# A sign step tied to its function table, two more parts of the second product in seven instead of eight, and a re-dated plan

## The chip, the cores and the metric

The program runs on one core of a Trainium2 chip. Its time is device microseconds of one execution, the median of several runs. A core has five engines that matter here: TensorE (PE, the matrix multiplier; PEld is its weight load), VectorE (DVE), ScalarE (ACT), GpSimd (POOL) and SyncE (SP), which issues the DMA transfers. Each executes its own instructions strictly in the order in which they were written down, and waits on semaphores of the others.

## The reference: what is computed

```python
# attention with random features, per batch b (8) and head (8): 576 tokens, 64 wide, 128 features
phi(x) = exp(proj - |x|^2/2 - max) / sqrt(m),  proj = x @ omega.T
kv  = phi(k).T @ v ;  z = sum of phi(k)
attn = (phi(q) @ kv) / (phi(q) @ z + 1e-6)          # -> x: 4608 tokens x 512
# feed-forward
h   = x @ w_in                                      # 512 -> 2048
g   = h * erf(softplus(h))
out = g @ w_out                                     # 2048 -> 512, float32
```

## The kernel before

**Precision.** The two products of the feed-forward part are done in a short float format whose rounding is undone by splitting: every operand is written as high + low, and each product is three matmuls (high·high, high·low, low·high).

**Tiling.** The 4608 tokens are cut into six groups ("supers", line 32, `SUPERS`): two of 2 x 288 tokens and four of 2 x 432. A super passes GEMM 1 (512 to 2048), the nonlinearity, and GEMM 2 (2048 to 512) in four parts q = 0..3 (`NQ`). A part has two granules of GEMM 1's output, each 4 blocks (two feature blocks by two token halves). The names of the trace: `h`, or `hX hY hZ`, are GEMM 1's accumulators, `hs` its output in SBUF, `gs` what softplus and erf make of it, `gh` and `gl` the high and low part of g, `o`, or `oX oY oZ`, GEMM 2's accumulators and `os` its sums. A digit pair behind a name, as in `o_2_3`, is the part and the output block.

**Seven or eight products.** A 2 x 2 block product takes eight products of blocks, or seven with sums of blocks made beforehand (`PRODUCTS`, the accumulators X, Y and Z). GEMM 1 uses eight in the two small supers and seven in the others. GEMM 2 uses seven where `blocked(b, q)` (line 69) says so: super `b` at or past `FIRST2[q]`, and not the last part of the last super. `FIRST2` is 3 for every q, so super 2 and the two small ones use eight. A part in seven products needs four sums of activations (`gsum`, tiles `gs<-hs,hs` and `gs<-hs,gs`), three and a half high/low splits of a granule (`bh bb th`, `bl bb tl`) where a part in eight needs two (`gh`, `gl`), and sums of weights. These are made once, by `make_sums` (tiles R, S, c), in the super ahead of `FIRST2[q]` (line 927: `if b == FIRST2[q] - 1`), stored to DRAM as `wdc`, and fetched as `wb<-wdc` with the plain weights `wb<-wdw`.

**Weights.** They come as 64-bit words and are decoded on the chip, 32 units of them, during the first small super and early in the second (`make`): `wload` (tile st), `pbias` (line 438) on ScalarE (tile wt: a Prelu that makes sign and exponent; "the sign step"), `ptail` and `pjoin` on VectorE, and the split into high and low (tile w).

**Nonlinearity.** `chain` writes for a part: softplus of two granules, erf of the two, and the gate (g = erf · h). ScalarE holds one function table at a time: softplus, erf, and exp with ln (attention) are three sets. So a part takes three table loads: softplus, erf, and exp again.

**What sets the order.** `build` lists all steps with their reads, writes, engines and estimated costs. `Plan.order` (line 150) plays them in estimated time and writes each engine's instructions down in the order found: of the ready steps of an engine, the one with the earliest date (`due`). A step's `set` names the table it needs; while a softplus–erf pair runs (`macro`, `lock`) no other step *with* a set is let in, but one without a set may be. `JITTER` moves the dates of all steps in a stretch of dates by a pseudo-random amount of an entry's size (`o.id` and the entry's number k are the seed). `LAG`, `AHEAD`, `DRAIN`, `DIVIDE`, `GATES`, `RESTS`, `LATE`, `SQA`, `WHG`, `FIRST` and `BY` are numbers by which dates and the choice of engine are set. All instructions carry the source line L1015 (L1047 in the changed kernel), the line of the recorder.

Of the kernel before, what the change touches and what calls it, by code (L numbers as in the profile page):

```python
# [20 lines left out]
B, H, S, D = 8, 8, 576, 64  # L21
# [41 lines left out]
            ("Y", "S4", "B22", (0, 1), 1),  # L63
            ("X", "A22", "T4", (1, 0), 0))

FIRST2 = (3, 3, 3, 3)


def blocked(b, q):

    return FIRST2[q] <= b < len(SUPERS) - (q == NQ - 1)


COST = dict(mm=0.132, proj=0.222, half=0.156, tr=0.109, kv=1.35, table=1.3)
BANDWIDTH = 270e3
LAG = {"T": 0.32725, "A": 0.2525, "V": 0.2605, "G": 0.3105, "S": 0.2904}
SLOTS = dict(w=8, g=11, u=2, f=2, mx=3, sq=3, v=1, qh=1, ql=1, kh=1, kl=1, xs=12, xh=2, xl=2,
             os=4, ps=8)
CAPS = dict(st=3, wt=1, ws=1, wp=2, cv=2, att=4, moe1=5, moe2=3, hs=4, gs=2, w=6, wsums=7)
# [26 lines left out]
class Plan:  # L106
# [43 lines left out]
    def order(self, slots, caps):  # L150
# [6 lines left out]
        for o in reversed(ops):  # L157
# [2 lines left out]
            for s in o.succ:  # L160
                due = min(due, s.due - dur - 0.4)
            o.due = due
        for k, (lo, hi, amp) in enumerate(JITTER):
            for o in ops:
                if lo <= o.due < hi:
                    o.due += amp * ((o.id * 7919 + k * 104729 + 17) % 1009 / 504.0 - 1.0)
# [45 lines left out]
        while True:  # L212
# [74 lines left out]
            while True:  # L287
                if kind == "idle":
                    idle[x] = True
                elif kind == "done":  # L290
                    for s in x.succ:
                        s.left -= 1
                        lag = 0.0 if x.eng != "S" and len(s.opts) == 1 and s.opts[0][0] == x.eng \
                            else LAG[x.eng]
                        s.ready = max(getattr(s, "ready", 0.0) if s.left >= 0 else 0.0, now + lag) \
                            if hasattr(s, "ready") else now + lag
                        if not s.left:
                            event(max(now, s.ready), "push", s)
                    event(now + LAG[x.eng], "free", x)
                elif kind == "free":  # L300
# [17 lines left out]
def whole_(n):  # L318
# [1 line left out]
    return n < WHOLE or WHOLE2[0] <= n < WHOLE2[1]  # L320


JITTER = ((0, 0, 0), (186.1, 206.1, 4), (0, 0, 0), (0, 0, 0), (0, 0, 0), (227.5, 727.5, 4),
          (648.5, 748.5, 1), (712.0, 762.0, 2), (574.9, 594.9, 8), (27.8, 47.8, 0.5), (390.5, 440.5, 8),
          (458.1, 558.1, 8), (876.3, 896.3, 2), (0, 0, 0), (616.6, 816.6, 1))
AHEAD = 40.56

SPANS = ((0, 288), (288, 288))

DRAIN = 2.0  # L330
DIVIDE = 4.0
WHOLE = 32
WHOLE2 = (0, 0)
LESS = []
ROWS = 8
PAIR = 8.0
FIRST = 11.5
LEAD = 30.0
START0 = 4 * FIRST + 5

GATES = 10.0
RESTS = 6.0
EARLY = (0, 0)
STARTS = ()
BY = 30.0
RPOOL = SPOOL = "g"
VOS = 5
TAIL = [("V", 0.69, -1e9)]
LATE = 40.0
LOADS = 1e9  # L350
GATES0 = 1e9
RESTS0 = 1e9
SQN = 4
SQG = -1e9
SQA = 4.0
WHG = 5.0
WBG = -1e9


def build(emit):  # L360
# [49 lines left out]
    def fetch(u, t, src, ks, n):  # L410
        pl.op("wfetch", [("S", 0.1, AHEAD)], lambda e: E.fetch(t.ap[:, ks[0]:ks[-1] + 1].bitcast(F32), src()),
              reads=[(stored[u], 0)], writes=[(t, (x, k)) for x in "hl" for k in ks],
              size=P * n * BW * 8)
# [17 lines left out]
    def make(u, t):  # L431

        nm = "_".join(str(c) for c in u)
        st = pl.tile("w", f"st{nm}", [P, HW, 2], I32, "st")
        pl.op("wload", [("S", 0.1, AHEAD)], lambda e: E.w_load(st, u),
              writes=[(st, "h"), (st, "l"), (t, "room")], size=P * HW * 8)
        w = pl.tile("ps", f"wt{nm}", [P, HW], I32, "wp")
        pl.op("pbias", [("A", 0.67, -1e9)], lambda e: E.w_bias(e, st, w),
              reads=[(st, "h")], writes=[(w, 0)])
        pl.op("ptail", TAIL, lambda e: E.w_tail(e, st), reads=[(st, "l")], writes=[(st, "l")])  # L440
        pl.op("pjoin", [("V", 0.68, -1e9)], lambda e: E.w_join(st, w), reads=[(st, "l"), (w, 0)],
              writes=[(w, 0)])
        parts(t, lambda: w.ap.bitcast(F32).rearrange("p (k c) -> p k c", k=2), [(w, 0)], True)
        store(u, t)

    def room():
        count[0] += 1
        if clock[0] < starts[SUMS]:
            return CAPS["w"]
        return CAPS["wsums"] if clock[0] < starts[max(SUMS + 1, *FIRST2)] else SLOTS["w"]  # L450

# [453 lines left out]
    def gemm2(b, q, et):  # L905
# [16 lines left out]
        def one(t, f):  # L922
            if not ops:
                ops.extend(pl.tile("ps", f"o{b}_{q}_{et}_{i}", [P, 512], F32, "moe2",
                                   6 if b == len(SUPERS) - 1 else None) for i in range(2))
                w.append(weights2(q // 2, et, q % 2))
                if b == FIRST2[q] - 1:
                    beside[q, et] = w[0]
# [448 lines left out]
```

## Time and profile before

| what | value |
|---|---|
| runs | 1026.77, 1027.0, 1029.63 us; median 1027.0 |
| profiled execution | 1027.2 us, span of its instructions 1025.4 us |
| granted TensorE clock, mean | 0.997 |
| busy share of PE, DVE, ACT, POOL | 98%, 78%, 67%, 60% |
| moved by DMA | 232.72 MB, mean 227 GB/s |

How to read it: a busy share is an average over the span, and ends of matmuls are modelled, so what PE loses is seen best in the waits listed against it and in the start-to-start distance of its matmuls. In the rows of a timeline the first number is the start in microseconds from the span's start, the second the time up to the end of the merged instructions, and the bracket the idle time before, with what ended it. In rows of windows the numbers are busy microseconds of PE, PEld, DVE, ACT and POOL (instructions in brackets), the granted clock, the DMA share and GB/s. In rows of groups the number behind the bar is busy time, and behind the comma the mean of one in ns.

By the trace the first small super's GEMM 1 runs from 46.3 to 172 us, the second's from 185 to 332 us, super 2 starts at 345.9 us with its `hX`, super 3's first `hX` is at 502.9 us, and super 2's last `o` matmul at 567 us.

### The profile page before, as it was taken

How to read it: one execution, taken by the hardware profiler on the slowest of the kernel's cores; microseconds unless marked ns; L12 is line 12 of the kernel's file. 1: busy time of each engine (PE TensorE's matmuls, PEld its weight loads, DVE VectorE, ACT ScalarE, POOL GpSimd, SP SyncE). 2: the span in 40 equal slices, each digit the busy share in tenths (PEclk: the TensorE clock that was granted, in tenths of full speed). 3: DMA queues.
4: the chain of work that ended last, by engine and by line, in shares of the span. 5: the costliest groups of instructions: out<-in, count | busy, mean ns of one | idle time of the engine just before them, and what ended most of it. 6: DMA issues, size and time to landing. Idle time of an engine off the chain costs nothing.

```text
span 1025.4 us, 19428 instructions
## 1 busy us (share of the span) xinstructions
PE 1003.5 (98%) x7132; PEld 932.8 (91%) x7132; DVE 795.0 (78%) x1284; ACT 688.5 (67%) x1295; POOL 612.9 (60%) x446
## 2 busy tenths in 40 slices
PE   8999999999999999999999999999999999999998
PEld 7799889999999999999999888989989999989997
DVE  5788878877876976677787987798887687678664
ACT  8988776787685774765768585677657655644650
POOL 3625443875567816455788356489884668957520
PEclk9999999999999999999999999999999999999999
DMA  8377776699686766676657866656786457686751
GB/s 229 90 267 237 255 239 244 240 320 307 218 298 205 255 213 220 225 243 202 223 187 277 280 224 214 226 199 212 246 278 223 164 185 227 219 288 219 230 180 70
DMA packets 99486, 232.72 MB, mean 227 GB/s; under 512 B 11200, under 2 KB 11712, under 8 KB 99392
## 3 DMA queue, kind: packets, MB, share of 16 engines
q1 hardware_dynamic: 99232, 231.42, 67.5%
q8 instruction: 57, 0.93, 0.4%
q14 instruction: 37, 0.30, 0.1%
q10 hardware_dynamic: 160, 0.07, 0.0%
HBM read 188.45 MB, written 42.99 MB: 226 GB/s over the span
## 4 chain that ended last, share of the span: by engine, by line
PE 84%; DVE 6%; issue 3%; ACT 2%; DMA 2%; POOL 1%; SPq 1%; POOLq 0%; DVEq 0%; ACTq 0%
PE o L1015 17%; PE hX L1015 13%; PE h L1015 10%; PE oX L1015 9%; PE hY L1015 6%; PE nd L1015 5%; PE oY L1015 4%; PE ppq L1015 4%; PE ppk L1015 4%; PE kvp L1015 4%; PE hZ L1015 3%; PE pt L1015 2%; PE oZ L1015 2%; DMA uq<-qT 1%; DVE gs L1015 1%
## 5 line engine op out<-in xcount | busy, mean ns | idle before, releaser
L1015 PE MATMUL o<-gh,w 128*128 128x288 f32 (+1 forms) x832 | 213.5, 329 | 0.6 <-DVE w L1015 0.6
L1015 POOL TENSOR_TENSOR hs<-gs,hs 128x864 f32<-128x864 f32 (+1 forms) x50 | 112.2, 2266 | 106.1 <-ACT gs L1015 85.2
L1015 PE MATMUL hX<-xh,wb 128*128 128x432 f32 x512 | 168.6, 369 | 2.4 <-ACT hs L1015 1.4
L1015 PEld LDWEIGHTS o<-gh,w 128*128 128x128 f32 x832 | 145.2, 188 | 6.4 <-DVE w L1015 1.2
L1015 PE MATMUL o<-gl,w 128*128 128x288 f32 (+1 forms) x416 | 132.9, 319 | 0.1
L1015 PE MATMUL h<-xh,w 128*128 128x288 f32 x512 | 127.9, 318 | 5.0 <-DVE w L1015 4.4
L1015 PEld LDWEIGHTS hX<-xh,wb 128*128 128x128 f32 x512 | 96.2, 188 | 8.6 <-ACT hs L1015 1.8
L1015 POOL TENSOR_TENSOR uq<-uq 128x288 f32<-128x288 f32 (+1 forms) x50 | 50.9, 1038 | 79.2 <-DMA uq<-qN 38.9
L1015 PEld LDWEIGHTS h<-xh,w 128*128 128x128 f32 x512 | 89.0, 193 | 9.5 <-DVE w L1015 5.6
L1015 ACT ACT_TABLE_LOAD x72 | 92.4, 1283 | 2.0 <-PEq L1368 0.7
L1015 PE MATMUL hX<-xl,wb 128*128 128x432 f32 x256 | 91.6, 358 | 0.0
L1015 ACT ACTIVATE fk<-ppk,mxk 128x128 f32<-128x128 f32 x288 | 81.2, 379 | 8.9 <-DVE mxk L1015 8.0
L1015 PE MATMUL hY<-xh,wb 128*128 128x432 f32 x256 | 84.8, 368 | 0.0
L1015 ACT ACTIVATE fq<-ppq,mxq 128x128 f32<-128x128 f32 x288 | 78.1, 386 | 8.2 <-DVE mxq L1015 7.9
L1015 PE MATMUL oX<-th,wb 128*128 128x432 f32 x264 | 82.9, 361 | 0.0
L1015 PEld LDWEIGHTS o<-gl,w 128*128 128x128 f32 x416 | 78.3, 188 | 2.7 <-DVE gl L1015 0.5
L1015 ACT ACTIVATE rc<-nd,eps 64x288 f32<-64x288 f32 x128 | 63.4, 496 | 25.2 <-PE nd L1015 22.2
L1015 ACT ACTIVATE hs<-hX 128x432 f32<-128x432 f32 x71 | 37.1, 529 | 63.2 <-PE hX L1015 62.3
L1015 PE MATMUL nd<-qh,kh 128*128 128x288 f32 x256 | 76.3, 410 | 1.9 <-DVE qh L1015 1.4
L1015 PE MATMUL h<-xl,w 128*128 128x288 f32 x256 | 76.9, 300 | 0.7 <-POOL xl L1015 0.7
L1015 DVE TENSOR_TENSOR xs<-nd,rc 64x288 f32<-64x288 f32 (+1 forms) x160 | 61.2, 393 | 16.6 <-ACT rc L1015 11.1
L1015 ACT ACTIVATE gs<-hs 128x1728 f32<-128x1728 f32 (+1 forms) x48 | 69.4, 1481 | 1.1 <-POOL bl L1015 0.8
(141 smaller groups left out, 2642.4 us busy)
## 6 DMA issues: line engine op xcount, KB each, us to landing
wb<-wdc SPq DMA_DIRECT2D x216, 256.0 KB, 3.6
wb<-wdw SPq DMA_DIRECT2D x162, 256.0 KB, 3.9
w<-wdw SPq DMA_DIRECT2D x52, 512.0 KB, 4.7
st<-w SPq DMA_DIRECT2D x32, 512.0 KB, 4.9
wdw<-w SPq DMA_DIRECT2D x32, 512.0 KB, 4.3
wdc<-c SPq DMA_DIRECT2D x32, 512.0 KB, 4.7
v<-vP SPq DMA_DIRECT2D x32, 325.0 KB, 5.2
uk<-kR SPq DMA_DIRECT2D x24, 320.0 KB, 3.9
```

The source lines that it names most:

```text
L1015: return tc.keep_in_program_order(method(*args, **kwargs))
```

## The change

Four things are changed.

1. `pbias` gets `set="exp"`: the planner now takes the Prelu as a step of the exp table, so it is not let in between softplus and erf.
2. `FIRST2` goes from (3, 3, 3, 3) to (3, 3, 2, 2): parts 2 and 3 of super 2 use seven products, and the weight sums of these two parts are made one super earlier.
3. `JITTER` goes from 15 entries (five of them empty) to 120, each with a seed of its own.
4. A dozen numbers of the planner move a little, `LATE` (40 to 52.68) and `SQA` (4 to 6) most.

```diff
-FIRST2 = (3, 3, 3, 3)
+FIRST2 = (3, 3, 2, 2)
...
-LAG = {"T": 0.32725, "A": 0.2525, "V": 0.2605, "G": 0.3105, "S": 0.2904}
+LAG = {"T": 0.33914999999999995, "A": 0.258, "V": 0.24975, "G": 0.2994, "S": 0.3024}
...
-        for k, (lo, hi, amp) in enumerate(JITTER):
+        for lo, hi, amp, k in JITTER:
             for o in ops:
                 if lo <= o.due < hi:
                     o.due += amp * ((o.id * 7919 + k * 104729 + 17) % 1009 / 504.0 - 1.0)
...
-JITTER = ((0, 0, 0), (186.1, 206.1, 4), (0, 0, 0), (0, 0, 0), (0, 0, 0), (227.5, 727.5, 4),
...
+JITTER = ((186.1, 206.1, 4, 581), (227.5, 727.5, 4, 5), (648.5, 748.5, 1, 6), (712.0, 762.0, 2, 7),
...
-AHEAD = 40.56
+AHEAD = 40.09
-DRAIN = 2.0
-DIVIDE = 4.0
+DRAIN = 2.08
+DIVIDE = 3.94
-FIRST = 11.5
+FIRST = 11.4
-GATES = 10.0
-RESTS = 6.0
+GATES = 8.94
+RESTS = 5.64
-BY = 30.0
+BY = 30.39
-LATE = 40.0
+LATE = 52.68
-SQA = 4.0
-WHG = 5.0
+SQA = 6.0
+WHG = 4.28
...
         pl.op("pbias", [("A", 0.67, -1e9)], lambda e: E.w_bias(e, st, w),
-              reads=[(st, "h")], writes=[(w, 0)])
+              reads=[(st, "h")], writes=[(w, 0)], set="exp")
```

The whole program is ordered anew by this. Counted over the program, PE has 24 matmuls fewer (480 matmuls `o` of 432 columns become 288, the `oX oY oZ` go from 924 to 1092), ScalarE has 68 table loads in place of 72, SP issues 28 more fetches `wb` of 256 KB and 8 fewer fetches `w<-wdw` of 512 KB.

Where the instructions stand, at the three places that the prediction speaks of:

**ScalarE, the softplus–erf chain of the third part of the first small super** (`gs_4`, `gs_5`; `wt` are sign steps, `fq` exponentials of attention, `qh` transposed features, `gh` the high split of g). Before:

```order
L1015 ACT_TABLE_LOAD
L1015 ACTIVATE gs_4_1779<-hs_1_0_1481 128x1152
L1015 ACT_TABLE_LOAD
L1015 ACTIVATE wt_0_3_1_1811<-st_0_3_1_1693 128x512
L1015 ACT_TABLE_LOAD
L1015 ACTIVATE gs_5_1780<-hs_1_1_1579 128x1152
L1015 ACTIVATE w_0_3_1_20_1694<-wt_0_3_1_1811 128x2x256
L1015 ACT_TABLE_LOAD
L1015 ACTIVATE gs_4_1779<-gs_4_1779 128x1152
L1015 ACTIVATE gs_5_1780<-gs_5_1780 128x1152
L1015 ACTIVATE wt_1_4_1885<-st_1_4_1764 128x512
```

In the change:

```order
L1047 ACT_TABLE_LOAD
L1047 ACTIVATE gs_4_1765<-hs_1_0_1562 128x1152
L1047 ACTIVATE gs_5_1766<-hs_1_1_1597 128x1152
L1047 ACT_TABLE_LOAD
L1047 ACTIVATE gs_4_1765<-gs_4_1765 128x1152
L1047 ACTIVATE gs_5_1766<-gs_5_1766 128x1152
L1047 ACT_TABLE_LOAD
L1047 ACTIVATE wt_0_3_1_1851<-st_0_3_1_1709 128x512
L1047 ACTIVATE fq_3_1696<-ppq_3_2_1679,mxq_3_1683 128x128 x3
L1047 ACTIVATE wt_1_4_1885<-st_1_4_1743 128x512
```

Two table loads, a sign step and a split are gone from between the two softplus; the sign step `wt_0_3_1` now stands behind the chain, ahead of `wt_1_4`.

**ScalarE, behind the chain before that one** (`gs_2`, `gs_3`, the second part of the first small super): from its last table load to the sign step `wt_1_2`. Before:

```order
L1015 ACT_TABLE_LOAD
L1015 ACTIVATE fq_2_1287<-ppq_2_1_1248,mxq_2_1259 128x128 x3
L1015 ACTIVATE fq_2_1287<-ppq_2_2_1255,mxq_2_1259 128x128 x3
L1015 ACTIVATE wt_1_1_1475<-st_1_1_1341 128x512
L1015 ACTIVATE wt_1_2_1483<-st_1_2_1385 128x512
```

In the change, from the second group of exponentials behind that load:

```order
L1047 ACTIVATE fq_2_1393<-ppq_2_1_1252,mxq_2_1309 128x128 x3
L1047 ACTIVATE wt_0_3_0_1422<-st_0_3_0_1190 128x512
L1047 ACTIVATE fq_2_1393<-ppq_2_2_1281,mxq_2_1309 128x128 x3
L1047 ACTIVATE wt_1_0_1437<-st_1_0_1270 128x512
L1047 ACTIVATE w_0_3_0_12_1191<-wt_0_3_0_1422 128x2x256
L1047 ACTIVATE qh_2_1451<-pt_2_0_1441 128x384
L1047 ACTIVATE fk_3_1457<-ppk_3_0_1404,mxk_3_1424 128x128 x3
L1047 ACTIVATE qh_2_1451<-pt_2_1_1461 128x384
L1047 ACTIVATE wt_1_1_1477<-st_1_1_1330 128x512
L1047 ACTIVATE fk_3_1457<-ppk_3_2_1426,mxk_3_1424 128x128 x3
L1047 ACTIVATE fk_3_1457<-ppk_3_1_1414,mxk_3_1424 128x128 x3
L1047 ACTIVATE wt_1_2_1522<-st_1_2_1446 128x512
```

The sign steps `wt_0_3_0` and `wt_1_0`, which stood inside the chain before, are now behind it, and with the exponentials of the next pair (`fk_3`) they stand ahead of `wt_1_2`.

**PE, in GEMM 2 of part 2 of super 2** (parts and supers counted from 0; the first product's rows). Before:

```order
L1015 MATMUL o_2_0_1_6210<-gh_4_5960,w_1_0_0_101_6046 128x432
L1015 MATMUL o_2_0_1_6210<-gl_4_5983,w_1_0_0_101_6046 128x432
L1015 MATMUL o_2_0_1_6210<-gh_4_5960,w_1_0_0_101_6046 128x432
L1015 MATMUL o_2_2_0_6217<-gh_4_5960,w_1_2_0_102_6091 128x432
L1015 MATMUL o_2_2_0_6217<-gl_4_5983,w_1_2_0_102_6091 128x432
L1015 MATMUL o_2_2_0_6217<-gh_4_5960,w_1_2_0_102_6091 128x432 x2
L1015 MATMUL o_2_2_0_6217<-gl_4_5983,w_1_2_0_102_6091 128x432
L1015 MATMUL o_2_2_0_6217<-gh_4_5960,w_1_2_0_102_6091 128x432
L1015 MATMUL o_2_2_0_6217<-gh_5_5993,w_1_2_0_102_6091 128x432
L1015 MATMUL o_2_2_0_6217<-gl_5_6018,w_1_2_0_102_6091 128x432
L1015 MATMUL o_2_2_0_6217<-gh_5_5993,w_1_2_0_102_6091 128x432
```

In the change:

```order
L1047 MATMUL oX_2_0_6261<-bb_2_6100,wb_6095 128x432 x6
L1047 MATMUL oX_2_1_6279<-bb_2_6100,wb_6095 128x432 x3
L1047 MATMUL nd_3_0_0_6285<-qh_3_6215,kh_3_5920 128x288
L1047 MATMUL oX_2_1_6279<-bb_2_6100,wb_6095 128x432 x3
L1047 MATMUL nd_3_1_0_6295<-qh_3_6215,kh_3_5920 128x288
L1047 MATMUL oY_2_0_6304<-th_2_0_6127,wb_6120 128x432
L1047 MATMUL oY_2_0_6304<-tl_2_0_6244,wb_6120 128x432
L1047 MATMUL oY_2_0_6304<-th_2_0_6127,wb_6120 128x432
L1047 MATMUL oY_2_1_6311<-th_2_0_6127,wb_6120 128x432
L1047 MATMUL oY_2_1_6311<-tl_2_0_6244,wb_6120 128x432
L1047 MATMUL oY_2_1_6311<-th_2_0_6127,wb_6120 128x432
```

What was a run over `gh`, `gl` with one unit of weights is now products X and Y on the sums `th` and the blocks `bb`, with fetched weight blocks `wb`.

More of the change, by code (lines that the diff above doesn't have):

```diff
@@ L320, in whole_ @@
     return n < WHOLE or WHOLE2[0] <= n < WHOLE2[1]
-JITTER = ((0, 0, 0), (186.1, 206.1, 4), (0, 0, 0), (0, 0, 0), (0, 0, 0), (227.5, 727.5, 4),
-          (648.5, 748.5, 1), (712.0, 762.0, 2), (574.9, 594.9, 8), (27.8, 47.8, 0.5), (390.5, 440.5, 8),
-          (458.1, 558.1, 8), (876.3, 896.3, 2), (0, 0, 0), (616.6, 816.6, 1))
-AHEAD = 40.56
+JITTER = ((186.1, 206.1, 4, 581), (227.5, 727.5, 4, 5), (648.5, 748.5, 1, 6), (712.0, 762.0, 2, 7),
[34 rows of a table added]
+AHEAD = 40.09
 SPANS = ((0, 288), (288, 288))
-DRAIN = 2.0
-DIVIDE = 4.0
+DRAIN = 2.08
+DIVIDE = 3.94
 WHOLE = 32
```

34 rows, old and new, of the table JITTER are left out of this document.

## The prediction

> **What bounds the kernel now.** I read the page first: the busy shares, and the count of ScalarE's table loads.
>
> ```profile
> span 1025.4 us, 19428 instructions
> PE 1003.5 (98%) x7132; PEld 932.8 (91%) x7132; DVE 795.0 (78%) x1284; ACT 688.5 (67%) x1295; POOL 612.9 (60%) x446
> L1015 ACT ACT_TABLE_LOAD x72 | 92.4, 1283 | 2.0 <-PEq L1368 0.7
> ```
>
> TensorE is the bound, and nothing else is near it on average. So time can be had in two ways: fewer matmuls, or less waiting of TensorE. Next come the waits of TensorE, those inside the stream of work:
>
> ```profile
> PE h L1015 <- DVE w L1015: 4.4, 4, 2.2
> PE pt L1015 <- DVE hs L1015: 1.9, 1, 1.9
> PE hX L1015 <- ACT hs L1015: 1.4, 1, 1.4
> PE hX L1015 <- DVE hs L1015: 1.0, 1, 1.0
> ```
>
> The largest sum, 4.4 us in four waits, is for weights just decoded; no wait for a fetched weight is in the list. The next three, 1.9, 1.4 and 1.0, are single waits late in the run. Windows around the weight waits show that they cost more than their length:
>
> ```profile
> 111.00:114.80 3.80, 1.42 (x11) 0.96 (x9) 3.77 (x8) 2.52 (x4) 3.27 (x3) 1.00 0.52 166
> 115.00:118.20 3.20, 3.20 (x14) 2.92 (x13) 3.13 (x5) 1.71 (x4) 3.20 (x4) 0.50 0.99 362
> 144.00:156.00 12.00, 8.56 (x63) 6.87 (x62) 11.36 (x15) 7.86 (x13) 10.73 (x8) 1.00 0.55 197
> 156.00:159.10 3.10, 3.10 (x14) 3.10 (x14) 2.96 (x8) 2.17 (x5) 0.15 (x1) 0.50 0.94 322
> ```
>
> TensorE lost 3.80 - 1.42 = 2.4 us at 111 us and 12.00 - 8.56 = 3.4 us at 144 to 156 us. Behind each place the granted clock is 0.50 over at least 3.1 to 3.2 us, in which half the work is done: another 1.6 us each. The two places cost 4.0 and 5.0 us.
>
> Why are the weights late there? ScalarE before the second place:
>
> ```profile
> 133.64 1.28 ACT L1015 ACT_TABLE_LOAD   x1
> ...
> 136.12 1.28 ACT L1015 ACT_TABLE_LOAD   x1
> 137.41 0.62 ACT L1015 ACTIVATE wt<-st 128x512 f32<-128x512 f32 x1
> 138.06 1.28 ACT L1015 ACT_TABLE_LOAD   x1
> 139.35 1.17 ACT L1015 ACTIVATE gs<-hs 128x1152 f32<-128x1152 f32 x1
> ...
> 141.02 1.28 ACT L1015 ACT_TABLE_LOAD   x1
> 142.32 2.23 ACT L1015 ACTIVATE gs<-gs 128x1152 f32<-128x1152 f32 x2
> 144.45 0.62 ACT L1015 ACTIVATE wt<-st 128x512 f32<-128x512 f32 x1
> 147.51 1.16 ACT L1015 ACTIVATE gh<-hs 128x1152 fp32r<-128x1152 f32 x1 [2.44 <-POOL hs L1015]
> ...
> 150.19 0.62 ACT L1015 ACTIVATE wt<-st 128x512 f32<-128x512 f32 x1
> ```
>
> A sign step (`wt<-st`) between the two softplus needs a table of its own: one load ahead of it at 136.12, one behind it at 138.06 to get softplus back. Everything behind it, erf, the gate on POOL, the splits `gh` and the next sign steps queued behind them, is 2.6 us later for these two loads. The same happens at 96.94 and 99.79 us, ahead of the first place. Four of the 72 loads are of this kind.
>
> **The change part by part.** The sum is made against the profiled execution, 1027.2 us (span 1025.4 and 1.8 around it); the median of the runs is 0.2 lower.
>
> *Seven products in two more parts.* What a 432-wide matmul costs, and how many there are:
>
> ```profile
> 1003.46 17.68 PE o L1015 x90
> L1015 PE MATMUL o<-gh,w 128*128 128x432 f32 x320 | 97.6, 368 | 0.0
> L1015 PE MATMUL o<-gl,w 128*128 128x432 f32 x160 | 57.4, 359 | 0.1
> ```
>
> 320 + 160 = 480 matmuls are five parts of 96. In seven products a part has 84. Two parts save 24, at 17.68 / 90 = 0.196 us each: **-4.7 us**, since TensorE hardly waits there (171 us of the stage, below).
>
> For it a part adds four sums, and three and a half splits for two. The nearest rows are
>
> ```profile
> L1015 DVE TENSOR_TENSOR gs<-hs,gs 128x864 f32<-128x864 f32 x17 | 30.3, 1780 | 4.7 <-POOL hs L1015 4.7
> L1015 POOL TENSOR_TENSOR c<-S,c 128x512 fp32r<-128x512 f32 x23 | 34.6, 1505 | 9.1 <-ACT c L1015 8.4
> 330.00:430.00 100.00, 100.00 (x714) 93.73 (x713) 78.64 (x124) 69.77 (x126) 53.87 (x40) 1.00 0.69 228
> 519.00:690.00 171.00, 170.92 (x1224) 154.54 (x1223) 141.80 (x233) 118.03 (x244) 107.94 (x80) 1.00 0.69 236
> ```
>
> Four sums at 1.8 us are 7 us; one and a half more splits, a high and a low of some 1.8 us each, 5.4: about 13 us a part, 25 in all, over three engines. They fall at the seam of super 2 and super 3, where the last row has DVE free for 29, ACT for 53 and POOL for 63 of 171 us. That stage carries four parts in seven products and twice super 2's attention already, and TensorE is busy in 170.92 of 171.00 us. So the average room is there. What such a part costs in waits I take from the whole run: three late waits of 1.9 + 1.4 + 1.0 = 4.3 us over the eleven parts done in this way (924 such matmuls by 84), 0.4 each, **+0.8 us** for two.
>
> The weight sums of the two parts move ahead, to the end of the second small super and the start of super 2: four groups of ten instructions. At no more than the 1.5 us of `c<-S,c` each, they take 60 us of the three engines; in 330 to 430 us these are free for 21 + 30 + 46 = 97 us of 300. I take nothing for it; if that cover failed, drains of TensorE's accumulators would queue behind them (below).
>
> Fetches: 28 x 0.262 - 8 x 0.524 = 3.1 MB more, 13 us of transfers at the stage's 236 GB/s, 8% of a stage in which the engines are 0.69 busy. They pass SP's queue ahead of the fetches of attention; TensorE waits for none of them now, and I cost them at nothing.
>
> *The sign step.* At the second place, the order of the change lets me add up ScalarE from the chain's first load to the sign step that came last there (`wt_1_6`): three loads 3.85, softplus 2 x 1.17, erf 2.23, four sign steps 2.5, three exponentials, two splits 2.3, two copies `qh`; with
>
> ```profile
> 93.55 0.88 ACT L1015 ACTIVATE fq<-ppq,mxq 128x128 f32<-128x128 f32 x3
> 94.45 1.28 ACT L1015 ACT_TABLE_LOAD   x1
> 109.10 1.27 ACT L1015 ACTIVATE wt<-st 128x512 f32<-128x512 f32 x2
> 112.35 0.53 ACT L1015 ACTIVATE qh<-pt 128x384 f32<-128x384 f32 x1
> ```
>
> 0.88 and 2 x 0.53 this is 15.2 us. Before it was 150.81 - 133.64 = 17.2. So the weights come 2.0 us sooner. TensorE comes later: its order there holds one more product of keys and values and six more transposes ahead of these weights,
>
> ```profile
> L1015 PE MATMUL kvp<-v,fk 128*64 128x65 f32 x1024 | 35.3, 221 | 0.0
> ```
>
> at least 35.3 / 32 = 1.1 us. Together 3.1 us of slack against 3.4 us of waits in four pieces. I take the waits as gone, and with them the slow stretch: **-5.0 us** (bounds 0 and -5.0).
>
> At the first place it is less clear. Two sign steps leave the chain, but are put behind it with more work (twelve rows of the order), so that `wt_1_2` ends some 19.3 us after the chain's first load, where it ended 110.4 - 94.5 = 15.9 us after it: three loads 3.85, softplus and erf 4.6, four sign steps 2.5, eighteen exponentials 5, and smaller ones 3.4. Against these 3.4 us stand five more attention products on TensorE ahead of `h_1_1` and an earlier start of the chain (sign step and two attention steps ahead of it instead of two weight steps and three exponentials, with their waits). By this about 1 us of the 2.4 stays, and the clock, which stayed at 1.00 after the late waits of 1.9, 1.4 and 1.0, would not drop. That gains 3.0; bounds 0 and -4.0. I take half, **-1.5 us**, since the order of VectorE and POOL has changed there too, and a step late on either would bring the wait back.
>
> By the Trainium skill (ScalarE: Activation LUTs, "What ACT_TABLE_LOAD costs") a change of set costs 1.28 us of load and about as much of drain, 2.66 in all. In the rows the sign step starts at 137.41, 1.29 us after its load: no drain shows. By the page's figure the first place would gain a further 2.7 us of slack and lose its rest, and the sum would be 1.5 lower; I go by the row.
>
> *Dates and numbers.* They reorder all engines and add no instruction. The late waits may go (-4.3) or others come (the last rival); the order tells no time, so I leave them as they are.
>
> Sum: -4.7 + 0.8 - 5.0 - 1.5 = -10.4; 1027.2 - 10.4 = 1016.8, against the median **1016.6 us**.
>
> **The rivals.**
>
> *The early waits only move* (chance 0.20). The sign steps now wait for the whole chain, so other weights are late, and the clock drops again. For it: at the first place ScalarE's path got longer. Against: at the second it got shorter, and four loads of 1.28 us are really gone. What stays is -4.7 + 0.8: 1023.1 us.
>
> *All waits go* (0.15). Both early places (-9.0) and the three late ones (-4.3) are cleared by the new order: 1027.0 - 4.7 - 9.0 - 4.3 = 1009.0. For it: PE's waits are few and small; against it: nothing in a row says that new dates fall better.
>
> *Drains held behind stretched VectorE instructions* (0.10). This one is slower. At the late wait of 1.9 us:
>
> ```profile
> 759.01 3.87 DVE L1015 TENSOR_TENSOR bl<-hs,bh 128x1728 fp32r<-128x1728 f32 x1
> 759.00 5.79 POOL L1015 TENSOR_TENSOR tl<-gs,th 128x864 fp32r<-128x864 f32 x2
> 1001.41 1.95 DVE L1015 TENSOR_TENSOR gl<-hs,gh 128x1728 fp32r<-128x1728 f32 x1
> ```
>
> A difference of two tiles takes VectorE 1.95 us alone and 3.87 with a like one on POOL; the drain that frees TensorE's bank stands behind it. If each of the thirteen parts met this once, it would be 13 x 1.9 = 25 us for the 4.3 (and 0.8) in the sum: 1016.6 + 20 = 1036.6 us. From some 18.6 us of it (1.4 a part) on the change is slower than can be told from noise. Against: three of eleven parts meet it now.
>
> By the Trainium skill (SBUF — State Buffer, "SBUF: two separate sides") the two engines share one pair of ports, locked for a whole instruction, and "the other fully blocks". The rows above agree, and it speaks against any change that adds two-input work to both, as this one does.
>
> That the change doesn't do what it says is no rival: 68 loads and 24 fewer matmuls stand in the order.
>
> **How the numbers follow.** Forecast 0.55, around 1016.6, own range 1012 to 1021. About 0.3% (3 us) can be told from no change in this kernel: under 1023.9 is faster, over 1030.1 slower. Faster: 0.54 of the forecast, 0.15, and 0.12 of the 0.20 at 1023.1: 0.81. Same: the rest of these, 0.01 + 0.08, and 0.03 of the slower rival's near end: 0.12. Slower: 0.07. The range leaves out the slower rival and half of the best case: 1009.5 to 1025.5.
>
> **What would show it.** In the profile of the change: 68 table loads; no granted 0.50 between 140 and 175 us (the second place), and at 105 to 120 us either none or a wait of about 1 us; `o` matmuls of 432 columns 192 and 96; TensorE's waits for `DVE w` under 1.5 us in sum; late waits for `hs` of 3 to 6 us. The prediction is wrong if the waits for `w` stay over 4 us, if TensorE waits for `wb` or for `hs` between 330 and 690 us, or if the late waits pass 10 us.

## The result, and the profile after

The changed kernel takes 1039.3 us (median of 4 runs, 1038.52 to 1040.37) against 1026.9 us: 1.0117 times as long, with an interval of 1.0095 to 1.0139. It is 12.4 us slower, and 22.7 us above the forecast. Its profiled execution is one of 1038.5 us, of which the program's span is 1036.7.

The first lines of the page show nothing of this. TensorE is as busy as before, on 24 matmuls fewer, and the four table loads are gone:

```profile
span 1036.7 us, 19484 instructions
PE 1003.6 (97%) x7108; PEld 931.0 (90%) x7108; DVE 807.2 (78%) x1290; ACT 684.2 (66%) x1299; POOL 639.1 (62%) x475
L1047 ACT ACT_TABLE_LOAD x68 | 87.2, 1283 | 2.0 <-PEq L1400 0.7
```

The largest waits of TensorE inside the stream of work (total, times, longest) do:

```profile
PE oX L1047 <- DVE os L1047: 8.2, 1, 8.2
PE pt L1047 <- ACT qh L1047: 2.9, 2, 2.4
PE o L1047 <- DVE w L1047: 2.8, 4, 1.7
PE o L1047 <- ACT w L1047: 2.4, 1, 2.4
PE pt L1047 <- ACT hs L1047: 1.8, 1, 1.8
PE o L1047 <- ACT qh L1047: 1.3, 1, 1.3
```

One wait of 8.2 us is new. The weights `w` are waited for 5.9 us in all, where before had 5.0, now mostly ahead of GEMM 2's matmuls (`o`) in place of GEMM 1's (`h`). Windows laid on the slow stretches (length, busy time of PE, PEld, DVE, ACT, POOL, then TensorE's granted clock) show what followed the waits:

```profile
107.90:114.75 6.85, 5.14 (x22) 5.14 (x23) 5.67 (x11) 3.67 (x12) 4.03 (x4) 0.50 0.92 331
227.40:230.80 3.40, 3.40 (x14) 3.12 (x14) 2.07 (x4) 3.32 (x11) 3.32 (x3) 0.50 1.04 381
512.40:517.50 5.10, 0.00 (x0) 0.00 (x0) 5.10 (x1) 0.84 (x4) 5.10 (x4) 1.00 0.38 124
517.50:524.35 6.85, 3.75 (x11) 3.03 (x13) 6.10 (x6) 0.00 (x0) 1.56 (x2) 0.50 0.03 5
725.75:732.55 6.80, 5.88 (x17) 5.28 (x18) 3.85 (x5) 4.67 (x10) 6.63 (x5) 0.50 0.30 109
```

Four stretches of work have a granted clock of 0.50, where before had two. Half of TensorE's busy time in them is lost: 2.6, 1.7, 1.9 and 2.9 us. With the waits summed in the same way, the whole difference can be added up by stage (the first 60 us, waits for the first loads, left out):

| us | waits before | after | lost at half clock before | after |
|---|---|---|---|---|
| 60 to 260 | 6.6 | 7.2 | 3.4 | 4.3 |
| 260 to 480 | 0 | 1.2 | 0 | 0 |
| 480 to 600 | 0 | 8.2 | 0 | 1.9 |
| 600 to the end | 4.3 | 6.1 | 0 | 2.9 |

That is 11.8 us more of waits and 5.7 more at half clock; less 4.7 for the matmuls, and 0.4 less at the start, it makes 12.4, where the spans of the two profiles differ by 11.3 (that the medians differ by 12.4 too is chance). In all 18 profiles of this case (the two kernels and the sixteen below) span, less waits, less half-clock loss, plus the 4.7 where the two parts are in seven products, is 1003.0 to 1006.9 us. So these three terms are what moves the time, to within 2 us.

**The wait of 8.2 us.** A drain is an instruction that reads an accumulator of TensorE out, so that TensorE can write it again. VectorE, GpSimd and TensorE from 506 us on (start, duration, what; the wait before it in brackets):

```profile
506.80 0.60 DVE L1047 TENSOR_TENSOR os<-oY,os 128x432 f32<-128x432 f32 x1
507.31 12.19 DVE L1047 TENSOR_TENSOR xl<-xs,xh 128x432 fp32r<-128x432 f32 x1
519.43 0.59 DVE L1047 TENSOR_TENSOR os<-oZ,os 128x432 f32<-128x432 f32 x1
519.95 0.59 DVE L1047 TENSOR_TENSOR os<-oX,os 128x432 f32<-128x432 f32 x1
507.06 1.14 POOL L1047 TENSOR_TENSOR xl<-xs,xh 128x432 fp32r<-128x432 f32 x1
508.16 1.66 POOL L1047 TENSOR_SCALAR xh<-xc 128x1728 fp32r<-128x1728 f32 x1
509.77 1.30 POOL L1047 TENSOR_TENSOR uq<-uq 128x288 f32<-128x288 f32 x2
511.02 1.13 POOL L1047 TENSOR_TENSOR xl<-xs,xh 128x432 fp32r<-128x432 f32 x1
512.10 3.98 POOL L1047 TENSOR_TENSOR hs<-gs,hs 128x864 f32<-128x864 f32 x2
516.02 2.15 POOL L1047 TENSOR_TENSOR gs<-hs 128x432 f32<-128x432 f32 x2
518.14 0.92 POOL L1047 TENSOR_SCALAR bb<-hs 128x864 fp32r<-128x864 f32 x1
520.60 0.73 PE L1047 MATMUL oX<-th,wb 128*128 128x432 f32 x1 [8.24 <-DVE os L1047]
```

A subtraction of 432 columns, some 0.6 us of work, takes VectorE 12.19 us; such an instruction is called held below. It is no late drain: the addition that frees `oX` is 0.59 us long and stands behind it. All the while GpSimd runs ten instructions without a gap, none of them longer than the mean of its group, and VectorE is done 0.45 us after the last of them ends (519.06). The groups of instructions have eight subtractions of this shape in both kernels, at 996 ns each before,

```profile
L1015 DVE TENSOR_TENSOR xl<-xs,xh 128x432 fp32r<-128x432 f32 x8 | 8.0, 996 | 0.0
```

and at 2630 now:

```profile
L1047 DVE TENSOR_TENSOR xl<-xs,xh 128x432 fp32r<-128x432 f32 x8 | 21.0, 2630 | 0.0
```

**The early waits.** ScalarE and TensorE at the first place:

```profile
98.47 2.22 ACT L1047 ACTIVATE gs<-gs 128x1152 f32<-128x1152 f32 x2
100.71 1.28 ACT L1047 ACT_TABLE_LOAD   x1
102.01 1.66 ACT L1047 ACTIVATE fq<-ppq,mxq 128x128 f32<-128x128 f32 x6
103.52 0.68 ACT L1047 ACTIVATE wt<-st 128x512 f32<-128x512 f32 x1
106.69 0.60 ACT L1047 ACTIVATE w<-wt 128x512 fp32r<-128x512 f32 x1 [1.16 <-DVE wt L1047]
107.34 0.40 PE L1047 MATMUL o<-gh,w 128*128 128x288 f32 x1 [2.41 <-ACT w L1047]
```

The sign step of GEMM 2's last weight stands behind the error function, the load and six exponentials, and TensorE waits for just this weight.

**The wait at 726 us.** ScalarE:

```profile
724.59 1.64 ACT L1047 ACTIVATE th<-gs 128x1728 fp32r<-128x1728 f32 x1 [2.13 <-POOL gs L1047]
726.14 0.47 ACT L1047 ACTIVATE qh<-pt 128x384 f32<-128x384 f32 x1
726.67 0.90 PE L1047 MATMUL pt<-ident,fq 128*128 128x128 f32 x3 [2.36 <-ACT qh L1047]
```

A rounding that waits for GpSimd stands ahead of a drain that TensorE needs.

### The profile page after: what moved, and what is told of

Same layout as the page of the kernel before. It is cut to its first block, busy times and chain, and to the rows that moved or that the text cites. A ratio compares the mean times of both kernels' runs of the same rounds, so it can differ in the third digit from the quotient of the medians.

```text
span 1036.7 us, 19484 instructions
## 1 busy us (share of the span) xinstructions
PE 1003.6 (97%) x7108; PEld 931.0 (90%) x7108; DVE 807.2 (78%) x1290; ACT 684.2 (66%) x1299; POOL 639.1 (62%) x475
## 4 chain that ended last, share of the span: by engine, by line
PE 79%; DVE 8%; POOL 5%; ACT 4%; issue 3%; DMA 1%; SPq 0%; DVEq 0%; ACTq 0%; POOLq 0%
PE o L1047 13%; PE hX L1047 13%; PE oX L1047 10%; PE h L1047 8%; PE hY L1047 6%; PE nd L1047 6%; PE oY L1047 5%; PE ppk L1047 4%; PE ppq L1047 4%; PE hZ L1047 3%; PE kvp L1047 3%; PE pt L1047 2%; PE oZ L1047 2%; POOL gs L1047 2%; ACT gs L1047 2%
## 5 line engine op out<-in xcount | busy, mean ns | idle before, releaser
L1047 PE MATMUL o<-gh,w 128*128 128x288 f32 (+1 forms) x704 | 177.0, 326 | 6.7 <-DVE w L1047 2.8
L1047 PE MATMUL hX<-xh,wb 128*128 128x432 f32 x512 | 173.6, 373 | 1.0 <-DVE hs L1047 0.7
L1047 POOL TENSOR_TENSOR hs<-gs,hs 128x864 f32<-128x864 f32 (+1 forms) x46 | 102.1, 2243 | 96.3 <-ACT gs L1047 93.0
L1047 PEld LDWEIGHTS o<-gh,w 128*128 128x128 f32 x704 | 123.8, 191 | 12.0 <-DVE w L1047 4.1
L1047 PE MATMUL h<-xh,w 128*128 128x288 f32 x512 | 122.3, 311 | 0.8 <-DVE w L1047 0.4
L1047 PE MATMUL o<-gl,w 128*128 128x288 f32 (+1 forms) x352 | 111.0, 315 | 0.0
L1047 PE MATMUL oX<-th,wb 128*128 128x432 f32 x312 | 102.5, 369 | 8.2 <-DVE os L1047 8.2
L1047 POOL TENSOR_TENSOR uq<-uq 128x288 f32<-128x288 f32 (+1 forms) x48 | 42.4, 904 | 72.0 <-DMA uq<-qN 51.1
L1047 DVE TENSOR_TENSOR os<-oX,os 128x432 f32<-128x432 f32 x86 | 51.1, 603 | 24.8 <-PE oX L1047 24.2
L1047 PEld LDWEIGHTS oX<-th,wb 128*128 128x128 f32 x312 | 59.1, 190 | 11.8 <-DVE os L1047 8.6
```

What stands on the lines that cost most here:

```text
L1047: return tc.keep_in_program_order(method(*args, **kwargs))
```

## The experiments

Sixteen kernels; waits and half clock are those of the profiled execution from 60 us on, summed as above: the waits up to 260 us and behind it, then the time lost at half clock. The last column is the longest VectorE instruction on data in SBUF, where it is over 4 us.

| kernel | us | ratio to before | waits to 260, behind | half clock | held |
|---|---|---|---|---|---|
| before | 1026.9 | 1 | 6.6, 4.3 | 3.4 | 5.5 |
| changed | 1039.3 | 1.0117 (1.0095 to 1.0139) | 7.2, 15.5 | 9.1 | 12.2 |
| e1 | 1034.9 | 1.0074 (1.0046 to 1.0102) | 7.2, 13.7 | 7.4 | 10.9 |
| e2 | 1033.9 | 1.0060 (1.0043 to 1.0078) | 7.2, 13.0 | 4.5 | 10.9 |
| e3 | 1034.9 | 1.0073 (1.0045 to 1.0101) | 5.8, 15.5 | 4.1 | 12.2 |
| e4 | 1030.0 | 1.0035 (1.0019 to 1.0050) | 5.8, 12.6 | 1.9 | 10.9 |
| e5 | 1029.7 | 1.0031 (1.0018 to 1.0044) | 6.9, 8.6 | 6.0 | 5.3 |
| e6 | 1023.1 | 0.9958 (0.9946 to 0.9971) | 5.8, 8.0 | 0 | 5.3 |
| e7 | 1029.8 | 1.0031 (1.0016 to 1.0045) | 7.2, 8.6 | 1.7 | |
| e8 | 1030.2 | 1.0035 (1.0022 to 1.0048) | 6.3, 8.6 | 5.1 | |
| e9 | 1042.4 | 1.0139 (1.0108 to 1.0169) | 7.3, 13.1 | 9.0 | 8.0 |
| e10 | 1039.9 | 1.0118 (1.0088 to 1.0148) | 10.4, 10.9 | 9.6 | |
| e11 | 1030.2 | 1.0022 (0.9997 to 1.0047) | 7.1, 11.3 | 3.4 | 5.7 |
| e12 | 1023.7 | 0.9970 (0.9952 to 0.9987) | 5.8, 7.0 | 0 | 5.3 |
| e13 | 1039.2 | 1.0134 (1.0107 to 1.0162) | 10.4, 9.8 | 6.4 | 7.0 |
| e14 | 1033.0 | 1.0071 (1.0043 to 1.0099) | 8.3, 9.0 | 4.7 | |
| e15 | 1036.8 | 1.0111 (1.0088 to 1.0135) | 6.9, 11.8 | 7.7 | |
| e16 | 1033.4 | 1.0087 (1.0059 to 1.0114) | 6.4, 7.7 | 1.7 | |

The first six and e12 keep the changed kernel's order and edit it by hand behind the planner (steps have numbers there); the others let the planner lay the list anew. A list is the order of instructions that the planner lays, and the table of dates is `JITTER`. Code cuts leave lines out at `...`; the cuts of e2, e3 and e12 show the order on ScalarE and not code.

### The held instruction: e1, e5

e1 gives the step to the other engine:

```diff
+    ENG = {2755: 'G'}
...
-        o.fn(o.eng)
+        o.fn(ENG.get(o.id, o.eng))
```

> The changed kernel's order, with one instruction on another engine: the 128x432 subtraction xl<-xs,xh that VectorE held for 12.19 us from 507.31 us is given to GpSimd, one more instruction in its queue. Theory A (one held instruction): the VectorE queue behind it stood still, TensorE waited 8.2 us for the addition that frees oX, and 6.83 us at half clock followed, 3.7 us of it busy and so 1.9 us lost. With the subtraction elsewhere all of that goes: 1039.3 - 8.2 - 1.9 = 1029, and no TensorE wait over 3 us between 500 and 530 us. Theory B (too much work for the small engines in this stretch, whichever instruction is last): another VectorE or GpSimd instruction is held in its place, a wait of 5 us or more turns up within 30 us, and the time stays at 1036 to 1040.

It took 1034.9, neither 1029 nor 1036. The next such instruction on VectorE, behind the two drains, was held instead:

```profile
509.01 0.61 DVE L1047 TENSOR_TENSOR os<-oX,os 128x432 f32<-128x432 f32 x1 [0.55 <-PE oX L1047]
509.54 10.88 DVE L1047 TENSOR_TENSOR xl<-xc,xh 128x1728 fp32r<-128x1728 f32 x1
520.34 0.59 DVE L1047 TENSOR_TENSOR os<-oX,os 128x432 f32<-128x432 f32 x1
```

TensorE waited 6.4 us, two drains later. So it is not the one instruction but the stretch, as theory B has it. At the place itself next to nothing was gained: 6.4 us of wait and 3.0 at half clock, against 8.2 and 1.9. In the profile 2.9 us more are half clock that did not come at 227 us (1.7) and came for one half as long at 725 us (1.2), behind nearly the same waits, so the 4.4 us by which the kernel is faster are not this edit's alone. e5 leaves both queues as they are and makes GpSimd stop once:

```diff
+    last = const.tile([P, 1], F32, name="last")
...
+        if o.id == 2576:
+            x = next(t for t in plan.ops[2771].uses if t.name == "xl3_1")
+            pool.tensor_scalar(last, x.ap[:, 3, 0:1].bitcast(F32), 1.0, 0.0, op0=ALU.mult, op1=ALU.add)
```

> The changed kernel with one instruction more: ahead of the gate hs<-gs,hs on GpSimd (512.1 us in the changed kernel) GpSimd copies one column of xl, which VectorE's second subtraction writes, and so waits there until VectorE has done both subtractions. The order of both queues is otherwise the same. Theory A (VectorE's instruction with two operands in SBUF was passed over and then got in only when GpSimd's queue ran dry, at 519.06 us): it gets in when GpSimd stops, at about 512.1 us, and is held some 5 us instead of 12.19; the additions behind it end at 513.7 us instead of 520.5, TensorE's wait of 8.2 us shrinks to about 1, and the half clock there goes: 1039.3 - 7.0 - 1.9 = 1030.4, although GpSimd starts its gate 3.6 us later. Rival (VectorE is held by something else, such as the transfers or the operands' place, for a time of its own): the subtraction still takes 10 us or more, GpSimd waits with it, and the time is 1039 to 1045.

It took 1029.7 us, as theory A has it. VectorE's subtraction is done at 513.48, 0.46 us after GpSimd's `xl` is over (513.02), and the drains follow:

```profile
508.17 5.31 DVE L1047 TENSOR_TENSOR xl<-xs,xh 128x432 fp32r<-128x432 f32 x1
513.92 0.59 DVE L1047 TENSOR_TENSOR os<-oX,os 128x432 f32<-128x432 f32 x1
511.90 1.12 POOL L1047 TENSOR_TENSOR xl<-xs,xh 128x432 fp32r<-128x432 f32 x1
516.47 0.19 POOL L1047 TENSOR_SCALAR last<-xl 128x1 f32<-128x1 f32 x1 [3.45 <-DVE xl L1047]
514.57 0.47 PE L1047 MATMUL oX<-th,wb 128*128 128x432 f32 x1 [1.35 <-DVE os L1047]
```

That VectorE is held by GpSimd's unbroken run, and until it breaks, is shown. The kernel is 9.6 us faster, where the place costs 10.1 in waits and clock; in the profile 6.9 us of wait and 1.9 of clock are gone at the place, and 1.2 of clock at 720 us. By the Trainium skill (SBUF — State Buffer, "SBUF: two separate sides") the one that starts first has the shared ports for a whole instruction and "the other fully blocks"; the rows agree. But the Trainium skill speaks there of one instruction, and here it was ten in a row.

### The other places by hand: e2, e3, e4, e6, e12

e2 is e1 with `th<-gs` (at 724.6 us) one drain later on ScalarE:

```diff
 ACTIVATE qh<-pt
-ACTIVATE th<-gs
 ACTIVATE qh<-pt
+ACTIVATE th<-gs
```

> As the run before (the subtraction on GpSimd), and on ScalarE one rounding th<-gs of super 3's part 2 (at 724.6 us, where ScalarE had waited for GpSimd's gs) is put behind one drain qh<-pt instead of ahead of it. Theory A: TensorE's 2.4 us wait for that drain at 726.7 us goes, and the 6.83 us at half clock with it, 5.9 us of it busy and so 2.9 us lost: 5.3 us under the run before, 1029 - 5.3 = 1024. Theory B: ScalarE is simply late here and the next drain waits in turn: a wait of over 1.5 us for qh or hs between 722 and 740 us remains, and the time is within 1.5 us of the run before.

It took 1033.9, 1.0 us under e1 (runs of 1031.2 to 1035.1, so hardly to be told from it) and within theory B's bound on the time. B's sign, a wait of over 1.5 us, did not come: the wait of 2.4 became one of 1.3 for the third `qh`, and the clock stayed at 1.00 there.

e3 moves the four steps of weight 0_3_0 (the two on ScalarE are shown) and, at the second place on VectorE, one rounding behind two steps of a weight:

```diff
 ACTIVATE gs<-gs
+ACTIVATE wt_0_3_0<-st_0_3_0
 ACTIVATE gs<-gs
+ACTIVATE w_0_3_0<-wt_0_3_0
 ACT_TABLE_LOAD
 ACTIVATE fq<-ppq,mxq
-ACTIVATE wt_0_3_0<-st_0_3_0
...
-ACTIVATE w_0_3_0<-wt_0_3_0
```

> The changed kernel, with the decode of the last GEMM 2 weight moved by hand at the two early places, and nothing else. First place: the sign step of weight 0_3_0 is put between super 0's two error functions on ScalarE, where the rule of the change keeps it out, and the three other steps of this weight follow it. Second place: the rounding gh<-hs of 1.93 us on VectorE is put behind the two VectorE steps of weight 1_3_1. Theory A (the rule set the sign step behind the whole chain of softplus and error function, and TensorE waits for that one weight): the waits of 4.1 us at 105 to 110 us and of 2.0 us at 224 to 227 us go, with 2.5 and 1.7 us lost at half clock: 1039.3 - 10.3 = 1029, and no granted 0.50 before 500 us. Rival (decoding is too slow there whatever comes first, so that the waits only move to the next weight, 1_0, as my second forecast said of this place): waits of 3 us or more for w or h remain before 125 us, half clock stays there, and the time is 1035 to 1039.

It took 1034.9 us, 4.4 us less, between the two. TensorE no longer waits for 0_3_0, but 0.7 us for `fk` at 107 us and 1.2 and 0.5 for the next weights, and at the second place 1.1 for `fk` and 0.8 for `os`: the early waits go from 7.2 to 5.8 only. The half clock before 260 us, 4.3 us, is gone as A said; no single wait there is over 1.3 us any more. That is most of the gain.

e4 has e2 and e3 together.

> All four edits of the three runs before in one kernel. Theory A (independent places): the sum, 1039.3 - 10.1 - 5.3 - 10.3 = 1013.6, or 1017 to 1019 where the first early place only moves in part. Theory B (the two more parts in seven products load the three small engines too much everywhere): the places fill up again, 1028 to 1036.

It took 1030.0 us: the gains of e2 and e3 add up (5.4 + 4.4 against 9.3 measured), so the places are independent, as theory A has it. Its sum did not come, since each edit gave less than the 10.1, 5.3 and 10.3 us that A had for it: 4.4, 1.0 and 4.4. The time is in B's range. e6 takes e5's stop in place of e1's exchange.

> The changed kernel with the edits of e3 (last weights earlier), the one drain ahead of the rounding of e2, and the one waiting column of e5 in place of the subtraction on GpSimd. Theory A: e4 had 1030.0 with a TensorE wait of 6.4 us left at 511 us and 6.83 us at half clock, of which 1.9 us were lost; with these gone but for about 1 us of wait: 1030.0 - 5.4 - 1.9 = 1022.7, under the kernel before. Theory B (the stretch fills up again behind another instruction): 1028 to 1031.

It took 1023.1 us. No stretch at half clock is left in its profile (mean clock 1.000), and **the kernel is faster than both**, at 0.9958 of the one before. e12 puts two roundings behind more drains (one is shown).

```diff
-ACTIVATE th_0_1<-gs
 ACTIVATE hs<-hX
+ACTIVATE th_0_1<-gs
```

> The kernel of e6 with two roundings th<-gs on ScalarE, which there wait 1.0 and 5.2 us for GpSimd's gs at 712 and 762 us, put behind the drains that stood next: the one at 712 us behind the third qh<-pt too, the one at 762 us behind hs<-hX. Theory A (a step that waits for GpSimd and stands ahead of a drain on ScalarE costs TensorE the wait of the drain): TensorE's waits of 1.3 us for qh at 715.6 and of 1.8 us for hs at 764.2 us go but for 0.4: 1023.1 - 2.7 = 1020.4. Rival (the later th makes its own readers late): as much wait comes back for th or tl within 40 us, 1022 to 1024.

It took 1023.7 us, which is no gain. The waits behind 260 us fell by 1.0, not 2.7; new ones of 1.2 and 0.7 us came at 716 and 721 us, the first for a drain behind the later `th`. The rival holds.

### The parts of the change: e7, e8, e11, e9, e10

First the two parts on the kernel before, with its dates, alone and together; then the changed kernel less one part:

```diff
+              reads=[(st, "h")], writes=[(w, 0)], set="exp")
```

> The kernel before with the first part of the change alone: the sign step declares that it wants the set of exponentials; dates, numbers and FIRST2 as before. By the prediction's sum: the second early place goes (-5.0) and the first in part (-1.5): 1026.9 - 6.5 = 1020.4. Rival (by e3: the rule itself puts the sign step of each GEMM 2's last weight behind the chain, so the early waits come back at other places): waits of w above 4 us before 260 us, 1025 to 1031. In both cases the list is laid anew from 100 us on, and a new stall somewhere can add to either.

It took 1029.8 us. The waits before 260 us did not go (6.6 and 7.2); three of the four longest are for GEMM 2's weights, at 105, 143 and 221 us. The half clock there went, and 4.3 us of waits came in the list behind. The rival holds.

```diff
+FIRST2 = (3, 3, 2, 2)
```

> The kernel before with the second part of the change alone: two more parts of GEMM 2 in seven products; no set for the sign step, dates and numbers as before, so that the list is the same up to where the two parts bring work in. By the prediction's sum: 24 fewer matmuls (-4.7) and 0.8 of late waits: 1026.9 - 3.9 = 1023.0. Rival (the sums and roundings of the two parts load GpSimd and VectorE between 450 and 900 us, the drains behind them come late, and with TensorE's waits the half clock comes): late waits of 8 us or more in all and half clock after 330 us, 1030 to 1037.

It took 1030.2 us, at the near end of the rival: the waits behind 260 us doubled from 4.3 to 8.6, with 1.7 lost at half clock at 525 us. (2.3 us more at the start are waits for the first loads; before, e8 and e16 have the same list there, with 6.0, 8.3 and 5.9 us.) How much of this is due to the two parts and how much to any new list, e8 cannot tell: e16, below, has 3.4 us more waits behind 260 us without them.

> The kernel before with the set rule and the two parts in seven products, but its own dates and numbers: the change without its third part. Theory A (each part costs by itself, as e7 with +2.9 and e8 with +3.2 measured): 1026.9 + 6.1 = 1033, and the third part then accounts for 6 of the 12.4 us. Rival (the list is what decides, and two lists laid under the same rules differ by 5 us and more): anything from 1024 to 1040, with stalls at places that neither e7 nor e8 has.

Here are both lines at once, and it took 1030.2 us. The costs of the two parts do not add up to 6.1; together they are 2 to 3 us, by the interval 0 to 5. So dates and numbers, the third and fourth items of the change, make some 9 of the 12.4 us.

```diff
-FIRST2 = (3, 3, 2, 2)
+FIRST2 = (3, 3, 3, 3)
```

> The changed kernel with FIRST2 back at (3, 3, 3, 3): the set rule and the new dates and numbers as changed, the two added parts plain again, the list laid anew from where they were. Theory A (the two added parts are what cost: in the changed kernel TensorE's waits and half clock after 260 us are 15.5 + 4.8 us against 4.3 in the kernel before, 16 more, for 4.7 saved): back to 1039.3 - 16 + 4.7 = 1028, with the early waits of 7.2 us as they are, and no instruction held over 6 us. Rival (the new dates and numbers cost by themselves): waits of 8 us or more after 260 us remain, 1034 to 1044.

It took 1042.4 us, as the rival has it. Without the two parts the changed kernel is 3 us slower and no faster, and another VectorE instruction, with one operand, is held by GpSimd from 611 to 619.6 us (TensorE waited 3.8 us for the copy behind it):

```profile
612.58 7.96 DVE L1047 CAST th<-gs 128x1728 fp32r<-128x1728 f32 x1
620.46 0.59 DVE L1047 COPY os<-oX 128x432 f32<-128x432 f32 x1
```

e10 takes `set="exp"` away again.

> The changed kernel without the set rule: the sign step may again stand anywhere on ScalarE; FIRST2, dates and numbers as changed; the list is laid anew from about 40 us on. Theory A (the rule puts the sign step of each last GEMM 2 weight behind the chain, by e3): no TensorE wait over 1 us for an o<-gh,w at 100 to 112 and 220 to 230 us, but waits for h<-xh,w in their place, 5 to 7 us in all before 260 us as in every kernel so far. Rival (the early waits come from the dates): the waits for o<-gh,w of 2 us and more stay at 105 and 224 us. The time hangs on the stalls of the new list after 260 us, 1026 to 1040, and decides nothing between them.

It took 1039.9 us. The wait for `o<-gh,w` at 105 us is gone, with 1.7 us for `h` at 111 us and 3.5 at 146 to 153 us back in its place; at 219 us the wait for `o<-gh,w` is 3.6 us, more than with the rule. The waits before 260 us are 10.4 us in all, where 5 to 7 were expected. So the rule made the first early wait, not the second, and taking it away does not make the kernel faster.

### Numbers, table or draw: e13 to e16

e13 has the old numbers under the new table of dates, e14 the new numbers under the old table. e15 and e16 change one entry:

```diff
-(279.9, 299.9, 8, 972)
+(279.9, 299.9, 8, 973)
```

> The changed kernel with the planner's numbers of the kernel before (lags, AHEAD, DRAIN, DIVIDE, FIRST, GATES, RESTS, BY, LATE, SQA, WHG); set rule, FIRST2 and the new table of moved dates as changed. Theory A (the numbers cost): about 1030, as e11. Theory B (the table costs): 1037 to 1043, as the changed kernel. Theory C (every list laid anew is a draw): anywhere from 1024 to 1043.

It took 1039.2 us, as theory B has it.

> The changed kernel with the table of moved dates of the kernel before (15 entries with their old seeds); set rule, FIRST2 and the new numbers as changed. Theory A (the numbers cost): 1037 to 1043. Theory B (the table costs): about 1030. Theory C: anywhere from 1024 to 1043.

It took 1033.0 us, between theories A and B and nearer to B; by the ratio 7 us above the kernel before.

> The changed kernel with the seed of one entry of the table of moved dates (279.9 to 299.9 us, amplitude 8) at 973 instead of 972, so that the list is the same to about 250 us and laid anew behind it. Theory A or B (the rules, numbers and table of the third part cost everywhere): 1036 to 1042, with waits and half clock after 260 us as large as the changed kernel's 15.5 + 4.8 us, at other places. Theory C (a draw, and the 12.19 us instruction its main part): 1024 to 1032, and no instruction held over 6 us.

It took 1036.8 us, within theory A's and B's range, and by the ratio within 1 us of the changed kernel. No instruction is held, and the waits behind 260 us are 11.8 us with 3.4 at half clock, less than the 15.5 and 4.8 that A and B had.

> The kernel before with one entry more in its table of moved dates (279.9 to 299.9 us, amplitude 8), so that the list is the same to about 260 us and laid anew behind it. Theory A or B: within 3 us of the kernel before, 1025 to 1030. Theory C (the list of the kernel before is one of the better draws, and any change of it loses that): 1030 to 1040, with waits of 10 us and more after 260 us against 4.3.

It took 1033.4 us, as theory C has it, but not with its sign: the waits behind 260 us are 7.7 us and not 10. (The profiled execution, of 1029.7 us, is the fastest of four.)

Sorted by the table of dates: the five lists laid under the new one take 1036.8 to 1042.4 us, the six under the old one (e16 with its one entry more) 1026.9 to 1033.4. With the numbers as they are, the table alone makes 5 us (e14 against the changed kernel) or 11.5 (e11 against e13), by the ratios; the numbers alone make nothing under the new table (e13) and some 5 under the old (e14 against e11, whose intervals just overlap). So theory B holds in the main. But theory C has its share: one more entry costs the kernel before 9 us by the ratio (runs of 1029.7 to 1036.1 us, so the figure is loose), and the five other lists laid under its table lie 2 to 9 us above it by theirs. e10 and e15 have no held instruction and are as slow as the changed kernel, with their waits elsewhere. Why lists under the new table have more waits (26 to 28.3 us over the whole run, against 16.9 to 25.3) these runs do not show. The five share most of one table, so whether 120 entries cost as such or this draw of them is a poor one stays open too.

## Why the prediction was wrong

- **Seven products, -4.7.** Right: 24 matmuls fewer; what is left of the span without waits and half-clock loss is 4.8 us shorter in the mean of the fourteen profiles with the two parts than in that of the four without.
- **Their cost in waits, +0.8.** Too small in e8, which has 4.3 us more waits behind 260 us and 1.7 lost at half clock, 6.0 in all. The step took an average over eleven parts that had been placed, and left out that a new list brings waits of its own (3.4 us in e16, without a new part). How the 6.0 divide is not shown; in the changed kernel's list the two parts cost nothing net (e9).
- **Weight sums and fetches at nothing.** Nearly right: waits between 260 and 480 us went from 0 to 1.2 us, for `kh` and `fq` on ScalarE, and TensorE waits for no `wb`.
- **Second early place, -5.0.** Right at the place (TensorE idle for 1.0 us between 144 and 156 us, clock 1.00 there) and wrong in the sum: 2.1 us of waits, where before had 0.6, and 1.7 of clock came at 224 to 231 us. Without the rule (e10) the wait there is longer still, 3.6 us.
- **First early place, -1.5.** Wrong in sign. It cost 4.0 and now 4.1 + 2.6, because the rule put the sign step of one more weight behind the whole chain (without the rule this wait is not there, e10); I followed `wt_1_2` only, and the weight that came late was 0_3_0. The rival that the early waits only move (0.20) described what happened to them: 6.6 + 3.4 before, 7.2 + 4.3 after.
- **Dates and numbers, "I leave them as they are".** This is the step that failed most: the two together cost about 9 us (e11 against the changed kernel), and the table of dates alone 5 to 11.5 by the ratios. A zero stood there for want of a row, and nothing in the range for it, though all engines were ordered anew by it. Its largest piece in this list is the held stretch at 507 us, 10.1 us.
- **The slower rival, 1036.6 (0.10).** Nearest in time and in kind: a VectorE instruction stretched by GpSimd, drains behind it. But its size was wrong, and that its time came near is luck: not 1.9 us in each of thirteen parts, but one instruction of 12.19 us at one place, with 8.2 us of wait and 1.9 of clock. The row of 3.87 us that I read was taken as the worst that could happen to one instruction; the profile before already had one of 5.48 us, which no wait followed and which I did not quote:

```profile
568.99 5.48 DVE L1015 TENSOR_TENSOR tl<-gs,th 128x1728 fp32r<-128x1728 f32 x1
566.02 5.04 POOL L1015 TENSOR_TENSOR bl<-hs,bh 128x864 fp32r<-128x864 f32 x2
571.02 1.64 POOL L1015 TENSOR_SCALAR th<-gs 128x1728 fp32r<-128x1728 f32 x1
```

- **What would show it.** 68 loads, no 0.50 between 140 and 175 us and the counts of `o` came out; the waits for `w` came to 5.9 us, over the 4 named as the sign of failure, and the late waits (14.3 us from 480 us on) over the 10.

## What to carry to other kernels

In a kernel whose busiest engine loses only 2% of its time to waits and half clock, as this one did, a new order can be the largest edit of all: price it with the spread of lists laid under the same rules, here 2 to 9 us upwards, and not at nothing. Read the longest instruction of each group, not its mean, and look where a VectorE instruction on SBUF meets an unbroken run of GpSimd with a drain queued behind it. One wait placed in GpSimd's queue made the kernel 9.6 us faster (e5), and seven steps moved by hand another 6.6 (e6).

## What was not expected of the hardware

- **GpSimd can keep VectorE out for many instructions.** In the two traces, before and after, an instruction of GpSimd ended 171 times with the next one following within 0.15 us, while VectorE was at least 0.1 us inside a two-operand instruction on SBUF tiles that went on for 0.1 us or more. In 161 cases VectorE was done before GpSimd's next instruction, so it got in. In ten it was not: nine are in the 12.19 us, one in the 5.48 us above, and in both VectorE was done only after GpSimd ran dry (as in the 10.88 us of e1). What decides the first miss these traces do not show.
- **The same waits do not always bring the same half clock.** The stretches are 3.41 us long or two or three times that, but where the program's end cuts them off. The waits between 60 and 260 us were the same in the changed kernel, e1 and e2 (7.2 us, at the same places), and cost 4.3, 2.7 and 1.5 us of clock there. By the Trainium skill (TensorE: Matmul & The Clock Gate, "Part 1: The HAM clock gate") activity is judged in free-running windows of 3413 ns, and this agrees. That half clock comes after an idle window, as the Trainium skill has it there, does not: in the 3.41 us ahead of the stretch at 114.93 us in the kernel before, TensorE was busy for 1.2 us.
